# Second channel mixing of the last four tails by seven block products, with the row sums on GpSimd

## The chip, the cores and the metric

The kernel runs on one core of a Trainium2 chip. Its time is the device time of one execution in microseconds, as the median of several runs. The engines are called PE (TensorE), DVE (VectorE), ACT (ScalarE), POOL (GpSimd) and SP (SyncE); the last issues transfers, and so do ACT and POOL. All times below that begin with 2 and have three digits before the point, such as 228.24, are microseconds from the start of the profiled execution.

## The reference

A linear attention is followed by an MLP mixer. Batch 8, 8 heads, 576 tokens, head size 64, so that a token has 512 channels; 256 token units, 1536 channel units.

```python
phi = lambda x: np.where(x > 0, x, np.exp(x) - 1.0) + 1.0
q_p, k_p = phi(q), phi(k)
kv = np.einsum('bhsd,bhse->bhde', k_p, v)
z = np.sum(k_p, axis=2)
x = np.einsum('bhsd,bhde->bhse', q_p, kv) / (np.einsum('bhsd,bhd->bhs', q_p, z)[..., None] + 1e-06)
x = x.transpose(0, 2, 1, 3).reshape(B, S, 512)
h = np.maximum(x.transpose(0, 2, 1) @ w_tok1, 0.0) @ w_tok2
u = x + h.transpose(0, 2, 1)
out = u + np.maximum(u @ w_ch1, 0.0) @ w_ch2        # the channel mixing
```

The change concerns the last product, `@ w_ch2`, for a part of the rows.

## The kernel before

**Tiles.** The 576 tokens of a batch are 64 groups of 9. Of each group 8 tokens go into four row tiles of 128 (`R = 4`), and the ninth, the *tail*, gives 64 rows for each batch; two batches make one tail tile of 128 rows. The batches are worked one after another, with PE kept on one while the other engines prepare the next. The last block is batch 7 together with the tails of the last four batches, 4 to 7: two tail tiles, numbered e = 0 (batches 4 and 5) and e = 1 (6 and 7).

**Channel mixing.** `wc1` and `wc2` hold the two weight matrices; `u` and `ut` are the rows and tails after the token mixing, `cr` the values after the ReLU, 12 blocks of 128 channel units (`NCH = 12`, `KH = 6`), `crp` those of the two tail tiles of the last block, laid over the first half of the free `cr[0]`. The results are read from PSUM by DVE, which adds `u` and writes float32 into `obuf`, eight slots of 512 columns given out in turn by `o_slots`; from there they go to `out`.

**Seven products in place of eight.** For a pair of row tiles `product(n, j, i)` uses Strassen's scheme in Winograd's form: rows in 2 parts, the 1536 units in 2 halves, columns in 2 halves. Each of the products 1 to 7 is six matmuls of 256 columns. Its left sides are the blocks of `cr` or one of four row sums (`winograd`, `row_sums`, kept in `sb`), its right sides blocks of `wc2` or the sums of weights `tb`, made long before. Products 1, 6, 7 and 4 add up in one PSUM bank (X), 5 and 3 in another (Y), 2 stands alone (Z); DVE reads the bank after each product and adds it into one quarter of the output, so that a product that adds into a bank has to wait until the read before it is done. For batch 7, j = 0 and j = 1 are its two pairs of row tiles. In the names of the sequence below, `p40` is product 4 of j = 0.

**The tails before.** `tail_third(e, third)` makes four of a tail tile's 12 matmuls of 512 columns; after the third third, DVE reads the bank once, and SP and ACT each store one batch's 64 rows.

**The order.** The last block is an order written out by hand, the string `SEQUENCE`: `last_block` walks it, and each engine gets its instructions in this order. In it `m` stands for a product of the first channel mixing of batch 7 (`mix_first`), `c` for a sixth of the first mixing of the tails (`mm3_tails`, L570, with its ReLU on ACT at L572), `r` for the four row sums of two blocks on DVE, `q` for a third of a tail and `p` for a product with its read and, where it completes something, its store:

```python
SEQUENCE = """... m23 c3 m27 r0 c4 m24 r2 c5 q00 p10 r4 q01 p20 q02 p60 q10 p50
    q11 p70 q12 p11 p30 p21 p40 p61 p51 p71 p31 p41"""
```

**The stores.** j = 0 is stored as a whole after p40, in two transfers of 256 KB, one from SP and one from ACT (L806); j = 1 in four quarters, after p21, p71, p31 and p41, each as two transfers of 64 KB (L803). The two tail tiles go out after q02 and q12, each as two transfers of 128 KB (L598).

Of the kernel before, what the change touches and what calls it, by code (L numbers as in the profile page):

```python
# [13 lines left out]
ALU = mybir.AluOpType  # L14
# [5 lines left out]
def kernel(  # L20
# [20 lines left out]
    nc = tc.nc  # L41

    B, H, S, D = q.shape
# [3 lines left out]
    R = 4  # L47
    R1 = R + 1
    T = 2 * R + 1
# [5 lines left out]
    NCH = DCH // 128  # L55
# [10 lines left out]
    def bank(at=None):  # L66
        if at is None:
            at, ring[1] = ring[1], (ring[1] + 1) % 4
        return psum[:, at]
# [10 lines left out]
    def const(name, shape, dt=BF16):  # L80
        return consts.tile(shape, dt, name=name, tag=name)
# [6 lines left out]
    wc2 = const("wc2", [128, NCH, DM])  # L88
# [11 lines left out]
    ut = [const(f"ut{i}", [128, DM]) for i in range(2)]  # L100
# [3 lines left out]
    cr = [const(f"cr{b}", [128, NCH, SM]) for b in range(2)]  # L104
# [9 lines left out]
    half = [slice(0, 64), slice(64, 128)]  # L114
# [6 lines left out]
    def after(ins, other):  # L121
        if other is not None:
            tc.add_manual_dep(ins.ins, other.ins.name, sync_dep, reason="order of transfers")
        return ins
# [15 lines left out]
    live = {}  # L140
    o_at = [0]

    def o_slots(m):
        at = o_at[0] if o_at[0] + m <= 8 else 0
        o_at[0] = (at + m) % 8
        return obuf[:, at:at + m]
# [405 lines left out]
    def mm3_tail(p, i):  # L552
# [10 lines left out]
    crp = cr[0].rearrange("p k s -> p (k s)")[:, 0:NCH * 256].rearrange(  # L563
        "p (h k e s) -> p h k e s", h=2, e=2, s=128)
# [21 lines left out]
        if kcs[-1] == NCH - 1 and not wait:  # L586
            mm4_end(p, t)

    def tail_third(e, third):
        ps = bank(2 + e)  # L590
        for kc in range(4 * third, 4 * third + 4):
            nc.tensor.matmul(out=ps, lhsT=crp[:, kc // 6, kc % 6, e], rhs=wc2[:, kc, :],  # L592
                             start=(kc == 0), stop=(kc == NCH - 1))
        if third == 2:
            o = o_slots(2)[:, 0]
            nc.vector.tensor_tensor(out=o, in0=ps, in1=ut[e], op=ALU.add)
            for b, queue in enumerate((nc.sync, nc.scalar)):
                queue.dma_start(out=outv[B - 4 + 2 * e + b, :, 2 * R], in_=o[half[b]])  # L598

    outv = out.rearrange("n (p t) d -> n p t d", t=T)  # L600

    def mm4_end(p, t):
# [25 lines left out]
    KH = NCH // 2  # L628

    def bf(nm, b, i):  # L630
        t = raw[nm, b].rearrange("p j f -> p (j f)").bitcast(BF16)
        return t[:, 1536 * i:1536 * (i + 1)]

    tb = [bf("k", 1, i).rearrange("p (k c) -> p k c", k=KH) for i in range(3)] + [
        bf("q", 1, 0).rearrange("p (k c) -> p k c", k=KH)]
    tf = raw["q", 1].rearrange("p j f -> p (j f)")[:, 768:2304].rearrange("p (k c) -> p k c", k=KH)
    sb = [(bf("v", 1, i) if i < 3 else bf("q", 1, 1)).rearrange("p (k j s) -> p k j s", k=KH, j=2)
          for i in range(4)]
# [4 lines left out]
    def wblock(i, j):  # L643
        return wc2[:, KH * i:KH * (i + 1), 256 * j:256 * (j + 1)]
# [14 lines left out]
    def ablock(n, i, e):  # L659
        return cr[n % 2].rearrange("p k (j e s) -> p k j e s", j=2, e=2)[:, KH * i:KH * (i + 1), :, e]  # L660

    def winograd(s_, a, which, ks):
        a11, a12, a21, a22 = [t[:, ks] for t in a]
        x_, y_, op = {1: (a21, a22, ALU.add), 2: (s_[0][:, ks], a11, ALU.subtract),
                      3: (a11, a21, ALU.subtract), 4: (a12, s_[1][:, ks], ALU.subtract)}[which]
        nc.vector.tensor_tensor(out=s_[which - 1][:, ks], in0=x_, in1=y_, op=op)  # L666

    def row_sums(n, which, k0, m):
        winograd(sb, [ablock(n, i, e) for e in range(2) for i in range(2)], which,
                 slice(k0, k0 + m))  # L670


# [68 lines left out]
    def mix_first(g, i):  # L741
        ps = bank({1: (1, 4, 7), 6: (1, 4, 7), 7: (1, 4, 7), 4: (1, 4, 7), 2: (0, 0, 0),
                   5: (5, 6, 5), 3: (5, 6, 5)}[i][g]).rearrange("p (j c) -> p j c", j=2)
        first = i in (1, 2, 5)
        lhs, rhs = {1: (cblock(0, 0), ublock(0, 0)), 2: (cblock(0, 1), ublock(1, 0)),
                    3: (sw[3], ublock(1, 1)), 4: (cblock(1, 1), tu[3]), 5: (sw[0], tu[0]),
                    6: (sw[1], tu[1]), 7: (sw[2], tu[2])}[i]
        for j in range(2):
            cs = slice(128 * (2 * g + j), 128 * (2 * g + j) + 128)
            for k_ in range(2):  # L750
                nc.tensor.matmul(out=ps[:, j], lhsT=lhs[:, k_, cs], rhs=rhs[:, :, k_],  # L751
                                 start=(first and j == 0 and k_ == 0), stop=(k_ == 1),
                                 skip_group_check=not first or j == 1)
        c1, c6, c5 = hold[g]
        dst = lambda m, e: cr[1][:, KH * m + 2 * g:KH * m + 2 * g + 2, HALF[e]]
        if i == 4:
            nc.scalar.activation(out=dst(1, 0), in_=ps, func=AF.Relu)
        elif i in (1, 6, 5):
            nc.scalar.copy(out={1: c1, 6: c6, 5: c5}[i], in_=ps)
        else:  # L760
            o, c = {2: (dst(0, 0), c1), 3: (dst(0, 1), c6), 7: (dst(1, 1), c5)}[i]
            add_relu(o, ps, c)

    HC = [slice(0, 256), slice(256, 512)]

    def product(n, j, i):
        b = n % 2
        a_ = lambda h, e: ablock(n, h, e)[:, :, j]
        s_ = lambda k_: sb[k_][:, :, j]
        lhs, rhs, tile_, first = {  # L770
            1: (a_(0, 0), wblock(0, 0), "X", True), 2: (a_(1, 0), wblock(1, 0), "Z", True),
            6: (s_(1), tb[1], "X", False), 5: (s_(0), tb[0], "Y", True),
            7: (s_(2), tb[2], "X", False), 4: (a_(1, 1), tb[3], "X", False),
            3: (s_(3), wblock(1, 1), "Y", False)}[i]
        ps = bank({"X": (0, 4), "Z": (6, 5), "Y": (1, 7)}[tile_][j])[:, 0:256]
        for k_ in range(KH):
            nc.tensor.matmul(out=ps, lhsT=lhs[:, k_], rhs=rhs[:, k_], start=(first and k_ == 0),  # L777
                             stop=(k_ == KH - 1), skip_group_check=not first)
        if i == 1:
            live["oj", j] = o_slots(2)  # L780
        o = live["oj", j]
        ur = lambda e, c: u[b][:, 2 * j + e, HC[c]]
        add = lambda e, c, x_, y_: nc.vector.tensor_tensor(out=o[:, e, HC[c]], in0=x_, in1=y_,
                                                           op=ALU.add)
        if i == 1:
            add(0, 0, ps, ur(0, 0))
        elif i == 2:
            add(0, 0, ps, o[:, 0, HC[0]])
        elif i == 6:
            add(0, 1, ps, ur(0, 1))  # L790
        elif i == 5:
            add(1, 1, ps, ur(1, 1))
        elif i == 7:
            add(1, 1, ps, o[:, 1, HC[1]])
        elif i == 4:
            add(1, 0, ps, ur(1, 0))
        elif i == 3:
            add(0, 1, ps, o[:, 0, HC[1]])
        queues = [nc.sync, nc.scalar]
        if j == 1 and i in (2, 7, 3, 4):  # L800
            d, cs = {2: (0, HC[0]), 7: (1, HC[1]), 3: (0, HC[1]), 4: (1, HC[0])}[i]
            for e in range(2):
                queues[e].dma_start(out=outv[n, :, 2 * (2 * j + d) + e, cs], in_=o[half[e], d, cs])  # L803
        elif i == 4:
            for e in range(2):
                queues[e].dma_start(out=outv[n, :, 4 * j + e:4 * j + e + 3:2], in_=o[half[e]])  # L806


    ORDER = [1, 2, 6, 5, 7, 3, 4]
# [26 lines left out]
    def pair_put(n):  # L836
        for e in range(2):
            nc.gpsimd.dma_start(out=outv[n, :, e:e + 7:2], in_=live["o4"][half[e]])

    SEQUENCE = """m01 m02 m11 m05 m15 m06 m12 c0 m21 m03 m16 m07 c1 m25 m13 m22 m17 m04 c2 m26 m14
        m23 c3 m27 r0 c4 m24 r2 c5 q00 p10 r4 q01 p20 q02 p60 q10 p50
        q11 p70 q12 p11 p30 p21 p40 p61 p51 p71 p31 p41"""

    def last_block(n):
        for e in SEQUENCE.split():
            a = [int(c) for c in e[1:]]
            if e[0] == "m":  # L850
                mix_first(*a)
                if e == "m02":
                    pair_end(n - 1, "X", 1, 0)
                    pair_put(n - 1)
            elif e[0] == "c":
                mm3_tails(*a)
            elif e[0] == "p":
                product(n, a[1], a[0])
            elif e[0] == "q":
                tail_third(*a)  # L860
            else:
                for which in range(1, 5):
                    row_sums(n, which, a[0], 2)
# [205 lines left out]
    first = steps(1)  # L1069
# [71 lines left out]
    for n in range(2, B - 1):  # L1141
        p, b = divmod(n, 2)
# [123 lines left out]
```

## Time and profile before

| | |
|---|---|
| median of 8 runs | 249.45 us (248.0 to 250.53) |
| the profiled execution's own time | 248.22 us |
| its span | 246.4 us |
| PE busy | 237.2 us (96%), 2432 matmuls |
| DVE busy | 190.4 us (77%) |
| ACT busy | 139.6 us (57%) |
| POOL busy | 70.8 us (29%) |
| granted PE clock in the last 20 us | 1.00 |
| matmul of 512 columns of `tail_third`, mean | 379 ns |
| matmul of 256 columns of `product`, mean | 272 to 273 ns |
| read of 512 columns, L596 | 692 ns |
| read of 256 columns, L783 | 424 ns |
| row sum of 512 elements on DVE, L666 | 418 to 424 ns |

The span is the time from the first to the last instruction; the execution's own time is 1.8 us longer. A share of busy time is an average over all stages, and matmuls overlap each other, so what one costs is read from the distance between groups of them and not from its mean duration. A line in which several engines are named can be read by columns: start, length, engine, line, operation, output and inputs, how often. In a table by stretches each engine has its busy time and, in brackets, its number of instructions; the granted clock, the busy share of the 16 transfer engines and the rate in GB/s stand at the end.

### The profile page before, as it was taken

The page shows a single profiled execution, that of the slowest core. Times are in us where ns is not written, and L with a number is a line of the kernel's source. Part 1 is how long each engine was busy: PE and PEld are TensorE (multiplying, and loading weights), DVE is VectorE, ACT ScalarE, POOL GpSimd, SP SyncE. Part 2 cuts the span into 40 slices and gives each one's busy share as a digit, 9 for nine tenths or more (in the row PEclk, how much of TensorE's full clock was granted, in tenths as well). Part 3 has the DMA queues.
Part 4 walks back from the last instruction along what each step waited for, and adds up shares of the span by engine and source line. Part 5 has one row for each costly group of instructions (what it writes and reads, how often), then busy time and mean ns, then how long its engine had stood idle before and what let it go on. Part 6 is the DMA issues. An engine that isn't in the chain of part 4 may idle for free.

```text
span 246.4 us, 5963 instructions
## 1 busy us (share of the span) xinstructions
PE 237.2 (96%) x2432; PEld 158.5 (64%) x2454; DVE 190.4 (77%) x330; ACT 139.6 (57%) x224; POOL 70.8 (29%) x84
## 2 busy tenths in 40 slices
PE   7799999999999999999999999999999999999993
PEld 3484455564868556775778445864577566888672
DVE  5955777899799899979894397759884879956753
ACT  4773790669774387736896178655852651266100
POOL 9770040296702700070004500150006700530000
PEclk9999999999999999999999999999999999999999
DMA  6999999999715996599949967799061702361036
GB/s 240 270 203 251 353 277 319 349 257 291 286 24 117 257 381 227 111 250 295 404 125 157 396 182 235 122 346 230 23 136 28 170 3 43 64 130 43 4 85 170
DMA packets 49771, 48.39 MB, mean 196 GB/s; under 512 B 30032, under 2 KB 35536, under 8 KB 49744
## 3 DMA queue, kind: packets, MB, share of 16 engines
q1 hardware_dynamic: 41648, 35.00, 48.0%
q0 software_dynamic: 7472, 12.22, 22.3%
q10 hardware_dynamic: 624, 0.79, 1.1%
q8 instruction: 19, 0.31, 0.6%
q14 instruction: 8, 0.07, 0.1%
HBM read 35.85 MB, written 9.44 MB: 184 GB/s over the span
## 4 chain that ended last, share of the span: by engine, by line
PE 82%; DMA 11%; POOL 3%; issue 1%; DVE 1%; SPq 0%; POOLq 0%
PE ps L823 23%; PE ps L543 21%; DMA wc<-in_moe_w_ch_dram 7%; PE ps L312 6%; PE ps L583 5%; DMA q_raw<-in_q_dram 5%; PE ps L325 4%; PE ps L723 4%; PE ps L751 4%; PE ps L777 4%; PE ps L557 2%; PE ps L570 2%; PE ps L592 2%; PE ps L261 2%; PE ps L191 2%
## 5 line engine op out<-in xcount | busy, mean ns | idle before, releaser
L543 PE MATMUL ps<-uT,wc 128*128 128x512 bf16 x284 | 66.5, 379 | 0.3 <-issue 0.2
L550 ACT ACTIVATE cr<-ps 128x512 bf16<-128x512 f32 x67 | 39.1, 600 | 34.0 <-PE ps L543 33.6
L543 PEld LDWEIGHTS <-wc 128*128 128x128 bf16 x288 | 27.4, 98 | 29.7 <-issue 0.9
L834 POOL TENSOR_TENSOR obuf<-obuf,q_raw 128x512 f32<-128x512 f32 x6 | 7.6, 1269 | 91.2 <-DVE obuf L832 58.6
L823 PE MATMUL ps<-k_raw,v_raw 128*128 128x256 bf16 x216 | 24.9, 273 | 0.0
L832 DVE TENSOR_TENSOR obuf<-ps,u 128x512 f32<-128x512 f32 x24 | 16.2, 687 | 10.4 <-PE ps L823 8.8
L823 PEld LDWEIGHTS <-cr 128*128 128x128 bf16 x216 | 21.1, 98 | 4.1
L823 PEld LDWEIGHTS <-v_raw 128*128 128x128 bf16 x216 | 21.1, 98 | 3.9 <-issue 0.4
L151 ACT ACTIVATE e<-q_raw 128x1152 bf16<-128x1152 f32 x16 | 18.2, 1160 | 7.5 <-DMA q_raw<-in_q_dram 7.5
L151 ACT ACTIVATE e<-k_raw 128x1152 bf16<-128x1152 f32 x16 | 18.2, 1164 | 3.5 <-DMA k_raw<-in_k_dram 3.3
L823 PE MATMUL ps<-wc,cr 128*128 128x256 bf16 x144 | 17.7, 273 | 0.0
L276 DVE TENSOR_TENSOR x<-ps,dens 128x768 bf16<-128x768 f32 x18 | 17.2, 954 | 0.4
L666 DVE TENSOR_TENSOR v_raw<-cr 128x768 bf16<-128x768 bf16 (+2 forms) x24 | 14.8, 619 | 3.2 <-ACT cr L729 2.1
L337 DVE TENSOR_TENSOR u<-ps,x 128x1024 bf16<-128x1024 f32 x12 | 14.6, 1220 | 1.3 <-PE ps L325 1.1
L312 PE MATMUL ps<-x,w 128*128 128x512 bf16 x49 | 13.3, 379 | 0.3
L176 ACT CAST vs<-v_raw 128x1152 bf16<-128x1152 f32 x12 | 13.5, 1160 | 0.0
L165 DVE TENSOR_TENSOR qp<-e,y 128x1152 bf16<-128x1152 bf16 x16 | 11.9, 755 | 1.8 <-ACT e L151 0.8
L157 DVE TENSOR_SCALAR y<-k_raw 128x1152 bf16<-128x1152 f32 x16 | 11.7, 764 | 2.0 <-DMA k_raw<-in_k_dram 1.9
L583 PE MATMUL ps<-wc,cr 128*128 128x512 bf16 x47 | 11.8, 379 | 0.4 <-DMA wc<-in_moe_w_ch_dram 0.3
L834 POOL TENSOR_TENSOR obuf<-obuf,part 128x512 f32<-128x512 f32 x6 | 7.7, 1275 | 15.7 <-DVE obuf L832 15.7
L325 PE MATMUL ps<-ar,w2p 128*128 128x512 bf16 x44 | 11.8, 379 | 0.3
L165 DVE TENSOR_TENSOR kp<-e,y 128x1152 bf16<-128x1152 bf16 x16 | 11.7, 750 | 0.5 <-ACT e L151 0.4
(178 smaller groups left out, 430.3 us busy)
## 6 DMA issues: line engine op xcount, KB each, us to landing
k_raw<-in_k_dram SPq DMA_DIRECT2D x16, 576.0 KB, 6.6
q_raw<-in_q_dram SPq DMA_DIRECT2D x16, 576.0 KB, 5.8
v_raw<-in_v_dram SPq DMA_DIRECT2D x14, 576.0 KB, 10.1
out_dram<-obuf POOLq DMA_DIRECT2D x12, 512.0 KB, 6.6
wc<-in_moe_w_ch_dram POOLq DMA_DIRECT2D x8, 384.0 KB, 10.2
out_dram<-obuf POOLq DMA_DIRECT2D x4, 256.0 KB, 5.1
cr<-in_v_dram POOLq DMA_DIRECT2D x2, 288.0 KB, 7.6
out_dram<-obuf POOLq DMA_DIRECT2D x4, 128.0 KB, 7.9
```

The source lines that it names most:

```text
L151: nc.scalar.activation(out=e, in_=f, func=AF.Exp)
L165: live["phi"] = nc.vector.tensor_tensor(out=dst.transpose([0, 2, 1, 3]), in0=e.rearrange("p (i t d) -> p i t d", i=nj, t=T), in1=y.rearran ...
L276: nc.vector.tensor_tensor(out=xv[:, :, rc0:rc0 + 3], in0=v_[m][:, :, k0:k0 + 6, 0:D].rearrange("p i (q a) d -> p i q a d", a=2), in1=den.r ...
L312: nc.tensor.matmul(out=ps[:, mt], lhsT=w1t[:, b, ms] if r == R else w1[:, r, ms], rhs=x[b][:, r, :], start=(r == 0), stop=(r == R))
L325: nc.tensor.matmul(out=ps[:, i], lhsT=w2v(kt, r, b), rhs=ar[b][:, kt, :], start=(kt == 0), stop=(kt == NT - 1 and not add))
L543: nc.tensor.matmul(out=ps, lhsT=wc1[:, kj, 128 * mc:128 * mc + 128], rhs=uTj[b][:, kj] if n < 2 else uT[b][:, :, kj], start=(kj == 0), sto ...
L550: nc.scalar.activation(out=cr[b][:, mc, :], in_=ps, func=AF.Relu)
L583: nc.tensor.matmul(out=ps, lhsT=crt[:, kc, :] if t == 8 else cr[b][:, kc, 128 * r:128 * r + 128], rhs=wc2[:, kc, :], start=(kc == 0), stop ...
L666: nc.vector.tensor_tensor(out=s_[which - 1][:, ks], in0=x_, in1=y_, op=op)
L823: nc.tensor.matmul(out=live[tile_][:, j], lhsT=lhs[:, k_], rhs=rhs[:, k_], start=(first and j == 0 and k_ == 0), stop=(k_ == KH - 1), skip ...
L832: nc.vector.tensor_tensor(out=o, in0=live[tile_], in1=u[n % 2][:, d::2, HC[c]], op=ALU.add)
L834: nc.gpsimd.tensor_tensor(out=o, in0=o, in1=part[i], op=ALU.add)
```

## The change

The two tail tiles of the last block are treated as one pair of row tiles: their second channel mixing is made by seven products of six matmuls of 256 columns, instead of two tiles of 12 matmuls of 512 columns. The four row sums (`ts`, of 768 elements each, laid over the second half of `cr[0]`) are made by POOL; the first of them waits for the last row sum of batch 7 on DVE. The X bank of the tails is bank 2, Y is 3 and Z is 7. Their results go into two `obuf` slots, and each tail tile is stored as before by two transfers of 128 KB, after products t3 (tile 0) and t4 (tile 1).

In the sequence, `P` is a product's matmuls alone, `R` its read and store, `p` both; `T`, `U` and `t` are the same for the tails' products, where `T10` is the first five and `T11` the sixth matmul of product 1; `s` stands for the four sums on POOL. `r4` now comes ahead of all of batch 7's products, and the reads of p10, p20, p11, p21, p50, p60, p51, p61 and p70 are placed by themselves. The tails' products 1 and 2 come first of all, the other five among the last eight of batch 7.

```diff
-    def tail_third(e, third):
-        ps = bank(2 + e)
-        for kc in range(4 * third, 4 * third + 4):
-            nc.tensor.matmul(out=ps, lhsT=crp[:, kc // 6, kc % 6, e], rhs=wc2[:, kc, :],
-                             start=(kc == 0), stop=(kc == NCH - 1))
-        if third == 2:
-            o = o_slots(2)[:, 0]
-            nc.vector.tensor_tensor(out=o, in0=ps, in1=ut[e], op=ALU.add)
-            for b, queue in enumerate((nc.sync, nc.scalar)):
-                queue.dma_start(out=outv[B - 4 + 2 * e + b, :, 2 * R], in_=o[half[b]])
...
-    def winograd(s_, a, which, ks):
+    def winograd(s_, a, which, ks, engine=nc.vector):
...
-        nc.vector.tensor_tensor(out=s_[which - 1][:, ks], in0=x_, in1=y_, op=op)
+        return engine.tensor_tensor(out=s_[which - 1][:, ks], in0=x_, in1=y_, op=op)
 
     def row_sums(n, which, k0, m):
-        winograd(sb, [ablock(n, i, e) for e in range(2) for i in range(2)], which,
+        live["row"] = winograd(sb, [ablock(n, i, e) for e in range(2) for i in range(2)], which,
                  slice(k0, k0 + m))
...
-        ps = bank({"X": (0, 4), "Z": (6, 5), "Y": (1, 7)}[tile_][j])[:, 0:256]
+        if first:
+            live[tile_, j] = bank({"X": (0, 4), "Z": (6, 5), "Y": (1, 7)}[tile_][j])[:, 0:256]
+        ps = live[tile_, j]
         for k_ in range(KH):
             nc.tensor.matmul(out=ps, lhsT=lhs[:, k_], rhs=rhs[:, k_], start=(first and k_ == 0),
                              stop=(k_ == KH - 1), skip_group_check=not first)
+
+    def product_read(n, j, i):
+        b = n % 2
+        ps = live[{2: "Z", 5: "Y", 3: "Y"}.get(i, "X"), j]
...
+    ta = [crp[:, h, :, e] for e in range(2) for h in range(2)]
+    ts = [cr[0].rearrange("p k s -> p (k s)")[:, 3072 + 768 * i:3840 + 768 * i].rearrange(
+        "p (k s) -> p k s", k=KH) for i in range(4)]
+
+    def tail_sums():
+        for which in range(1, 5):
+            after(winograd(ts, ta, which, slice(0, KH), nc.gpsimd),
+                  live["row"] if which == 1 else None)
+
+    def tail_product(i, ks):
+        lhs, rhs, tile_, first = {
+            1: (ta[0], wblock(0, 0), 2, True), 2: (ta[1], wblock(1, 0), 7, True),
+            6: (ts[1], tb[1], 2, False), 5: (ts[0], tb[0], 3, True), 7: (ts[2], tb[2], 2, False),
+            4: (ta[3], tb[3], 2, False), 3: (ts[3], wblock(1, 1), 3, False)}[i]
+        if ks[0] == 0 and first:
+            live["t", tile_] = bank(tile_)[:, 0:256]
+        ps = live["t", tile_]
+        for k_ in ks:
+            nc.tensor.matmul(out=ps, lhsT=lhs[:, k_], rhs=rhs[:, k_], start=(first and k_ == 0),
+                             stop=(k_ == KH - 1), skip_group_check=not first)
+
+    def tail_read(i):
+        ps = live["t", {1: 2, 2: 7, 5: 3, 3: 3}.get(i, 2)]
+        if i == 1:
+            live["ot"] = o_slots(2)
+        o = live["ot"]
+        e, c, x_ = {1: (0, 0, ut[0]), 2: (0, 0, None), 6: (0, 1, ut[0]), 5: (1, 1, ut[1]),
+                    7: (1, 1, None), 4: (1, 0, ut[1]), 3: (0, 1, None)}[i]
+        nc.vector.tensor_tensor(out=o[:, e, HC[c]], in0=ps,
+                                in1=o[:, e, HC[c]] if x_ is None else x_[:, HC[c]], op=ALU.add)
+        if i in (3, 4):
+            for b, queue in enumerate((nc.sync, nc.scalar)):
+                queue.dma_start(out=outv[B - 4 + 2 * e + b, :, 2 * R], in_=o[half[b], e])
...
-        m23 c3 m27 r0 c4 m24 r2 c5 q00 p10 r4 q01 p20 q02 p60 q10 p50
-        q11 p70 q12 p11 p30 p21 p40 p61 p51 p71 p31 p41"""
+        m23 c3 m27 r0 c4 m24 r2 c5 T10 T20 T11 T21 r4 s P10 R10 P20 P11 P21 P50 U1 U2 R11 P60 R60
+        P51 R50 P61 R20 R21 P70 R51 R61 R70 p30 t6 p71 t5 t7 p40 p31 t3 t4 p41"""
```

`product_read` holds what `product` did after its matmuls, unchanged; in the changed kernel the store of a quarter of j = 1 is line 798, that of j = 0 line 801 and that of a tail tile line 837.

More of the change, by code (lines that the diff above doesn't have):

```diff
@@ L856, in last_block @@
                 mm3_tails(*a)
[L857 to L860, printed above, removed]
+            elif e[0] in "pPR":
+                if e[0] != "R":
+                    product(n, a[1], a[0])
+                if e[0] != "P":
+                    product_read(n, a[1], a[0])
+            elif e[0] in "tTU":
+                if e[0] != "U":
+                    tail_product(a[0], (range(KH - 1), range(KH - 1, KH))[a[1]] if a[1:] else range(KH))
+                if e[0] != "T":
+                    tail_read(a[0])
+            elif e[0] == "s":
+                tail_sums()
             else:
```

## The prediction

> **What bounds the kernel now.** I read the page first (slices, then the chain), then the chain over the last 10 us, and then the output transfers, because the change touches only the last stage. The rows of the slices are tenths busy in 40 equal slices of 6.16 us.
>
> ```profile
> PE   7799999999999999999999999999999999999993
> DMA  6999999999715996599949967799061702361036
> ```
>
> TensorE (PE) is full to the last slice, and the transfer engines, nearly idle around 230 us, are busy again at the very end. The chain of waits, in order of time (start, length, what):
>
> ```profile
> 227.37 0.87 PE ps L570 x8
> ...
> 229.76 0.86 PE ps L592 x4
> 230.63 0.65 PE ps L777 x6
> ...
> 236.70 5.95 PE ps L777 x54
> 242.65 0.02 issue
> 242.67 0.42 DVE obuf L783
> ```
>
> The last mixing of the tails' first layer (L570) ends at 227.37 + 0.87 = 228.24. From there PE runs without a gap to 242.65. A third of a tail (four matmuls of 512 columns, L592) costs 0.86; a product of six matmuls of 256 columns (L777) costs 5.95 / 9 = 0.661. Check: 14 x 0.661 + 6 x 0.86 = 14.41 = 242.65 - 228.24. The last read ends at 243.09, but the span is 246.44: 3.35 us are output transfers and the close. So I look at those: the timeline of the two issuing queues, the issues with their time to landing, what moved in two stretches, and which queue moved it.
>
> ```profile
> 239.16 0.50 ACTq L803 DMA_DIRECT2D out_dram<-obuf  x1
> 239.81 0.73 ACTq L806 DMA_DIRECT2D out_dram<-obuf  x1
> 241.80 2.06 ACTq L803 DMA_DIRECT2D out_dram<-obuf  x3
> ```
>
> ```profile
> out_dram<-obuf ACTq DMA_DIRECT2D x4, 64.0 KB, 2.4
> out_dram<-obuf SPq DMA_DIRECT2D x1, 256.0 KB, 3.2
> out_dram<-obuf ACTq DMA_DIRECT2D x1, 256.0 KB, 4.1
> ```
>
> ```profile
> 241.00:243.25 2.25, 1.64 (x15) 1.19 (x13) 1.37 (x4) 0.00 (x0) 0.00 (x0) 1.00 0.91 220
> 243.25:245.00 1.75, 0.00 (x0) 0.00 (x0) 0.00 (x0) 0.00 (x0) 0.00 (x0) 1.00 0.81 241
> ```
>
> The last two columns are the busy share of the 16 transfer engines and GB/s. Row block j = 0 leaves in one piece after product p40 (2 x 256 KB, issued at 239.81). Its data moves for 2.25 us at 0.91 busy; then the three last quarters of j = 1 (p71, p31, p41; 2 x 64 KB each) move until 245.0. Between 241.1 and 242.4, and again between 242.7 and 243.3, one queue alone is served:
>
> ```profile
> q1 hardware_dynamic: 121, 0.25, 94.9%
> ```
>
> ```profile
> q10 hardware_dynamic: 91, 0.17, 93.1%
> ```
>
> Hence ScalarE's half of p40 (q10) lands 4.1 us after its issue, SyncE's half (q1) after 3.2. So the present end is balanced: PE sets when p41 is issued (243.1 to 243.3), and the transfer engines are just free when it arrives.
>
> **What the Trainium skill says.** "VectorE: DVE Perf Modes", the section on the errata, prices a matmul at 6 + columns cycles of 2.4 GHz: 216 ns for 512, 109 for 256; the trace has 0.86 / 4 = 215 and 0.661 / 6 = 110. "DMA: Bandwidth & Descriptors", Queues, rings and completion order: an engine finishes a packet of one queue before it turns to the next queue; the q1-then-q10 lines agree. "GPSIMD Engine Reference", Key points: GpSimd shares its SBUF interfaces with VectorE, with contention where VectorE has two SBUF inputs. The row sums of VectorE have two, but they end before the new sums start; the product reads have one PSUM and one SBUF input. No trace line here shows such a slowdown.
>
> **PE.** Removed: 24 matmuls of 512 columns, 6 x 0.86 = 5.16. Added: 7 products of 256, 7 x 0.661 = 4.63. All of it lies on the path: -0.53. Twenty-one products from 228.24 end at 242.12. The k-th ends at 228.24 + 0.661 k: p70 is 11th, t6 13th (starts 236.17), p71 14th, t5 15th, t7 16th, p40 17th (239.48), p31 18th, t3 19th (starts 240.14), t4 20th, p41 21st. The first two tail products are split so that block 5, whose ReLU ends about 228.9, is wanted at 229.3: no wait.
>
> **VectorE.** r4's four row sums move ahead of the first reads. Groups follow each other by 1.46 (r0 226.64, r2 228.10), so r4 runs from 229.6 to 231.1; p50, the first user, starts at 232.2. Two 512-column reads of 0.69 become seven of 0.42 (+1.56 busy). Walking the new order at 0.35 to 0.45 per read, R60 waits for its product until 233.6, R70 starts at 235.8, and from p30 on each read follows its product by about 0.1. Every product that adds into a bank finds its read done: p70 (starts 234.85) needs R60, done 234.05, the closest. Cost 0; the cover is 0.8.
>
> **GpSimd.** Four sums of 768 bf16 elements. No such row exists; two neighbours do:
>
> ```profile
> L694 POOL TENSOR_TENSOR k_raw<-wc 128x256 bf16<-128x256 bf16 x6 | 3.8, 668 | 0.0
> ...
> L653 POOL TENSOR_TENSOR k_raw<-wc,q_raw 128x512 bf16<-128x512 bf16 x3 | 3.4, 1170 | 0.0
> ```
>
> Slope 1.96 ns per element, so 1.67 each; started at 231.2 they end at 232.9, 234.6, 236.2, 237.9. Wanted: the second at 236.17, the third at 238.16, the fourth at 240.14. Slack 1.6 or more, cost 0; nothing else stands on GpSimd's queue then. Bounds: 0, and, if each took the longest L653 (1.67 against 1.17, so 2.4), t3 would stall 0.7. Stalls begin at 2.23 each.
>
> **The output transfers.** The tail rows leave before as 2 x 128 KB at 232.9 and again at 237.1, in idle queues. Now they leave at the end. Issues from the reads (product end + 0.1 + 0.42): p21 235.2, p71 238.0, p40 240.03 (was 239.81, +0.22), p31 240.7, t3 241.35, t4 242.0, p41 242.6. From p40 on that is 512 + 128 + 256 + 256 + 128 KB = 1.31 MB instead of 0.92.
> *Pile-up.* p40's data begins 1.25 after issue (as now) and takes 2.25: to 243.55. Behind it stand 0.79 MB. At 241 GB/s that is 3.25, to 246.8; at full share (241 / 0.81 = 298) 2.64, to 246.2. Now data ends at 245.0, so +1.2 to +1.8.
> *A wait on a counter.* The built program's order names, for every DMA of SyncE and ScalarE, one of eight counters taken in turn, and a DMA first waits for the DMA that had its counter before. On ScalarE:
>
> ```
> before: 128 KB c1, 128 KB c3, p21 c5, p40 c7, p71 c1, p31 c3, p41 c5
> after:  p21 c1, p71 c3, p40 c5, p31 c7, t3 c1, t4 c3, p41 c5
> ```
>
> p41 waited for p21, long landed; now it waits for p40. p40's ScalarE half lands at 240.03 + 4.1 = 244.1, so p41 is issued there at 244.15 instead of 243.3: +0.85. Nothing is queued behind it but the close. Its data would come 1.25 later, at 245.4, into the backlog. The two mechanisms overlap, they don't add: the later one rules. Bounds for the end: +0.85 (queues as fast as they ever were) and +2.1 (p40's second half delayed too, by p31 and t3 on the other queue). I take +1.4.
>
> **The sum.** PE's -0.53 is gained but only brings p41's read to 242.5, ahead of a wait. Data ends at 246.4, the span about 247.85, against 246.44 and the profiled run's 248.22, so 249.6 for such a run. That run lies 1.2 below the median of 8 (249.45); on the median the change gives 250.85.
>
> **Rivals.**
> *The PE gain arrives.* If p40 lands within 2.6 us (its halves served side by side), p41 is issued at 242.6 on both queues and the queue is empty by 244.2: end -0.5, 248.95. For it: PE is full, and 0.53 is certain. Against: one queue at a time was served, and 4.1 is measured. It decides once p40 lands by about 243.4, the time at which p41 was issued before; anything earlier is no slower than before.
> *Only the counter wait.* The transfer engines drain 0.79 MB at the speed of the last stretch without its gaps and p41 is just late by its wait: +0.85, 250.3.
> *GpSimd late, or p40's second half late.* Sums of 2.4 stall t3 by 0.7 and push t3, t4 and p41 together; or p40's q10 half lands 0.8 later and takes p41 with it: +2.1, 251.55.
>
> **How the numbers follow.** Pile-up with the wait 0.60 (own range 250.4 to 251.3), only the wait 0.17, the PE gain 0.10, the late case 0.13. The likeliest gives 250.85. Leaving out the PE gain and the top of the late case, about 2 in 10, gives 249.95 to 251.7. Half a per cent, about what a measurement here can tell from none, is 1.25: slower than 250.70 is 0.65 of the first (0.39), nearly all of the late case (0.12) and a little of the second (0.02): 0.53. Faster than 248.20 would need more than PE has to give: 0.02. Between: 0.45.
>
> **What would show it.** In the new profile: 54 and more matmuls without a gap ending near 242.1; the last read near 242.5; ScalarE's last issue of line 798 at 244.1 or later though its data was ready at 242.6; the engines near 0.9 busy from 241.3 to past 246; GpSimd sums of 1.7 and no PE wait on them. Wrong, if ScalarE's p41 is issued at 242.7 and the span is below 246.4, if the busy stretch ends by 245.2, or if PE shows a hole before t6, t7 or t3.

## The result, and the profile after

The changed kernel took 250.19 us (median of 19 runs, 249.16 to 251.24), the kernel before 249.0 us in the same comparison (median of 52 runs). The ratio is 1.0053, with a 95% interval of 1.0037 to 1.0069: slower by half a per cent, some 1.3 us. The profiled execution took 250.27 us, its span is 248.5 us.

Part of the difference between the two spans (2.04 us) has nothing to do with the change. The chain of waits of the changed kernel, in order of time:

```profile
228.17 0.87 PE ps L570 x8
229.04 1.31 PE ps L823 x12
230.35 6.55 PE ps L768 x60
...
242.15 0.67 PE ps L768 x6
242.81 0.02 issue
242.84 0.42 DVE obuf L778
```

The tails' first layer ends at 229.04, in the kernel before at 228.24. Up to there both execute the same instructions. In twelve profiled executions, one for each kernel of the table below, the point lies between 227.93 and 229.46, and it does not follow the kernel: e1 and e2, which differ from the changed kernel only in the stores of the tails, have it at 228.24 and 228.15. In the profile of the changed kernel the shift arises at 83 us, where PE waits 0.86 for a transfer (`uT<-u`) for which it does not wait in the profile of before; in e3 and e5 it is there within the first 50 us. So I measure from this point: its distance to the end of the span, called the *stretch* below. It is 18.20 before and 19.44 after: +1.24, about what the ratio says (0.53% of 249.0 are 1.32).

PE is faster: 21 products take 242.82 - 229.04 = 13.78 where 14 products and six thirds took 14.41, without a hole. But between its last matmul and the end lie 5.66 instead of 3.79. The output transfers tell why. The issues on ScalarE's queue, with start and length:

```profile
240.68 0.68 ACTq L801 DMA_DIRECT2D out_dram<-obuf  x1
241.45 1.16 ACTq L798 DMA_DIRECT2D out_dram<-obuf  x1
242.70 1.97 ACTq L837 DMA_DIRECT2D out_dram<-obuf  x2
245.21 0.47 ACTq L798 DMA_DIRECT2D out_dram<-obuf  x1
```

These are p40, p31, the two tails (t3, t4) and p41. The read of p41 ended at 243.26; ScalarE issued its half at 245.21, two microseconds later. p40's half had landed just then, at 240.68 + 4.5:

```profile
out_dram<-obuf ACTq DMA_DIRECT2D x1, 256.0 KB, 4.5
```

And the transfer engines had no pause. The table by stretches (the last two columns are their busy share and GB/s):

```profile
242.00:243.00 1.00, 0.80 (x8) 0.47 (x5) 0.59 (x2) 0.00 (x0) 0.00 (x0) 1.00 0.95 195
243.00:244.00 1.00, 0.00 (x0) 0.00 (x0) 0.26 (x1) 0.00 (x0) 0.00 (x0) 1.00 1.00 259
244.00:245.00 1.00, 0.00 (x0) 0.00 (x0) 0.00 (x0) 0.00 (x0) 0.00 (x0) 1.00 0.88 263
245.00:246.00 1.00, 0.00 (x0) 0.00 (x0) 0.00 (x0) 0.00 (x0) 0.00 (x0) 1.00 0.99 328
246.00:247.00 1.00, 0.00 (x0) 0.00 (x0) 0.00 (x0) 0.00 (x0) 0.00 (x0) 1.00 0.78 258
```

So both mechanisms that were forecast are in the trace at once: p41 waits, and the engines are full while it waits. One profile can't say which of them costs the time. GpSimd's sums are no part of it:

```profile
232.06 6.55 POOL L655 TENSOR_TENSOR cr<-cr 128x768 bf16<-128x768 bf16 x4 [13.24 <-DVE q_raw L655]
```

The fourth ends at 238.6; t3, its first user, starts at 240.84, and no product of the chain waits for GpSimd.

### The profile page after: what moved, and what is told of

Read it like the earlier page. It is cut to its first block, busy times and chain, and to the rows that moved or that the text cites. A ratio compares the mean times of both kernels' runs of the same rounds, so it can differ in the third digit from the quotient of the medians.

```text
span 248.5 us, 6016 instructions
## 1 busy us (share of the span) xinstructions
PE 237.1 (95%) x2452; PEld 160.2 (64%) x2472; DVE 191.4 (77%) x335; ACT 139.7 (56%) x224; POOL 77.1 (31%) x88
## 4 chain that ended last, share of the span: by engine, by line
PE 64%; DVE 3%; DMA 2%; issue 1%; DVEq 0%
PE ps L854 19%; PE ps L543 17%; PE ps L312 4%; PE ps L712 4%; PE ps L740 4%; PE ps L768 4%; PE ps L325 3%; PE ps L570 2%; DMA uT<-u 2%; PE ps L823 2%; PE ps L261 1%; PE ps L191 1%; PE ps L557 1%; PE ps L583 1%; DVE u L337 1%
## 5 line engine op out<-in xcount | busy, mean ns | idle before, releaser
L863 DVE TENSOR_TENSOR obuf<-ps,u 128x512 f32<-128x512 f32 x24 | 16.2, 687 | 10.4 <-PE ps L854 8.8
L151 ACT ACTIVATE e<-q_raw 128x1152 bf16<-128x1152 f32 x16 | 18.3, 1162 | 6.3 <-DVE den L241 5.1
L151 ACT ACTIVATE e<-k_raw 128x1152 bf16<-128x1152 f32 x16 | 18.2, 1164 | 3.6 <-DMA k_raw<-in_k_dram 3.5
L325 PE MATMUL ps<-ar,w2p 128*128 128x512 bf16 x44 | 11.8, 379 | 0.3
L157 DVE TENSOR_SCALAR y<-q_raw 128x1152 bf16<-128x1152 f32 x16 | 12.0, 765 | 0.0
```

Of the source, the lines that this page charges most:

```text
L151: nc.scalar.activation(out=e, in_=f, func=AF.Exp)
L157: nc.vector.tensor_scalar(out=y, in0=f, scalar1=1.0, scalar2=1.0, op0=ALU.add, op1=ALU.max)
L325: nc.tensor.matmul(out=ps[:, i], lhsT=w2v(kt, r, b), rhs=ar[b][:, kt, :], start=(kt == 0), stop=(kt == NT - 1 and not add))
L863: nc.vector.tensor_tensor(out=o, in0=live[tile_], in1=u[n % 2][:, d::2, HC[c]], op=ALU.add)
```

## The experiments

All numbers of the last stage side by side. "PE" is the time from the end of the tails' first layer to PE's last matmul, "rest" from there to the end of the span; both from one profile each. The ratio is against the kernel before, over many runs.

| kernel | stretch | PE | rest | ratio (95% interval) |
|---|---|---|---|---|
| before | 18.20 | 14.41 | 3.79 | 1 |
| after | 19.44 | 13.78 | 5.66 | 1.0053 (1.0037 to 1.0069) |
| e1 no counter wait | 19.37 | 13.77 | 5.60 | 1.0064 (1.0040 to 1.0088) |
| e2 few bytes | 19.11 | 13.77 | 5.34 | 1.0036 (1.0020 to 1.0053) |
| e3 both | 18.20 | 13.78 | 4.42 | 1.0008 (0.9993 to 1.0023) |
| e4 p40 early | 18.12 | 13.77 | 4.35 | 1.0023 (1.0005 to 1.0041) |
| e5 before, tails late | 19.72 | 14.40 | 5.32 | 1.0060 (1.0039 to 1.0080) |
| e6 e4 with few bytes | 17.68 | 13.77 | 3.91 | 0.9998 (0.9976 to 1.0019) |
| e7 rows | 17.55 | 13.81 | 3.74 | 0.9982 (0.9966 to 0.9998) |
| e8 reads in line | 20.30 | 14.58 | 5.72 | 1.0085 (1.0051 to 1.0120) |
| e9 e3, GpSimd issues | 18.96 | 13.77 | 5.19 | 1.0030 (1.0014 to 1.0046) |
| e10 e7, GpSimd issues | 17.98 | 13.81 | 4.17 | 0.9995 (0.9982 to 1.0009) |

Each stretch is one profile. In the five kernels with the order of the change (after, e1, e2, e3, e9) ScalarE's half of p40 landed 4.4 to 4.5 after its issue, so a difference of 0.07 between two stretches is not told from none. The ratios hold the chance of the earlier stages too. And four of them hold one thing more: in every run of e4, e6, e7 and e10 the execution's own time is 2.1 us longer than its span (2.08 to 2.21), in every run of the other kernels 1.8 (1.73 to 1.86). So some 0.35 us, or 0.14%, of what these four gain in the stretch is lost outside the span; the runs do not show what it is. The mechanisms are read from the stretch, what a kernel is worth from the ratio.

**e1, the counter wait taken away, the bytes kept.**

```diff
-            for b, queue in enumerate((nc.sync, nc.scalar)):
-                queue.dma_start(out=outv[B - 4 + 2 * e + b, :, 2 * R], in_=o[half[b], e])
+            r0 = 64 * (B - 4 + 2 * e)
+            (nc.sync, nc.scalar)[e].dma_start(
+                out=out.rearrange("n (p t) d -> (n p) t d", t=T)[r0:r0 + 128, 2 * R], in_=o[:, e])
```

> The changed kernel, with each tail tile stored by one transfer of 256 KB (tile 0 from SyncE, tile 1 from ScalarE) instead of two of 128 KB. The same bytes at the same places, two issues fewer, so that p41 gets the counters of p71, which has long landed, and no longer those of p40. Theory A (pile-up: the transfer engines have no gap from p40's data on, and the bytes behind it set the end): p41 is issued about 1 us earlier but its data is not, the end stays, ratio to before 1.004 to 1.006 as for the change. Theory B (the counter wait sets the end): p41's data comes earlier, ratio 1.002 or less.

Measured: stretch 19.37, ratio 1.0064. On ScalarE:

```profile
241.90 1.33 ACTq L837 DMA_DIRECT2D out_dram<-obuf  x1
243.32 0.66 ACTq L798 DMA_DIRECT2D out_dram<-obuf  x1
```

p41 goes out at 243.32 - 228.24 = 15.08 after the first layer (16.17 in the changed kernel, 15.06 before), and the end comes only 0.07 earlier in the profile, and no earlier by the ratio, because the engines are full:

```profile
243.00:244.00 1.00, 0.00 (x0) 0.00 (x0) 0.00 (x0) 0.00 (x0) 0.00 (x0) 1.00 0.92 279
244.00:245.00 1.00, 0.00 (x0) 0.00 (x0) 0.00 (x0) 0.00 (x0) 0.00 (x0) 0.97 1.04 374
```

As theory A said: without the wait, the backlog alone keeps the end where it was.

**e2, the bytes taken away, the counter wait kept.**

```diff
-                queue.dma_start(out=outv[B - 4 + 2 * e + b, :, 2 * R], in_=o[half[b], e])
+                queue.dma_start(out=outv[B - 4 + 2 * e + b, :, 2 * R, 256 - 256 * e:264 - 256 * e],
+                                in_=o[half[b], e, 256 - 256 * e:264 - 256 * e])
```

> The changed kernel, with only 8 columns of each tail row stored after t3 and t4 (the other 504 columns of the tail rows are left out of the output): as many transfers and the same counters, but 0.5 MB less to move behind p40. Theory A (pile-up): the backlog is gone and PE's gain shows, ratio about 0.998, span some 0.5 below before. Theory B (counter wait): ScalarE's p41 is still issued only when p40 has landed, 4.1 to 4.5 after p40's issue, ratio 1.002 to 1.004.

Measured: stretch 19.11, ratio 1.0036. p41 is issued at 244.26 - 228.15 = 16.11, as in the changed kernel, and now the transfer engines run empty while it waits (0.30 busy in the last row):

```profile
243.00:244.00 1.00, 0.00 (x0) 0.00 (x0) 0.00 (x0) 0.00 (x0) 0.00 (x0) 1.00 0.80 231
244.00:245.00 1.00, 0.00 (x0) 0.00 (x0) 0.00 (x0) 0.00 (x0) 0.00 (x0) 0.53 0.30 53
```

As theory B said. Each mechanism is nearly enough by itself: taking one away gains 0.07 or 0.33, since the other holds the end.

**e3, both taken away** (one transfer for each tile, 8 columns of it).

> Both edits: one transfer for each tail tile and only 8 columns of it stored (the other 504 columns of the tail rows are left out). Neither backlog nor counter wait. Both theories: PE's gain of 0.5 to 0.6 shows in full, ratio 0.997 to 0.999. If it is 1.002 or more, the loss is not in the stores but in PE, VectorE or GpSimd.

Measured: stretch 18.20, ratio 1.0008: 1.24 gained, where the single edits give 0.40 in sum. But the expected PE gain of 0.6 isn't there: the rest is 4.42, not 3.79. On ScalarE:

```profile
241.82 1.15 ACTq L798 DMA_DIRECT2D out_dram<-obuf  x1
243.06 1.31 ACTq L837 DMA_DIRECT2D out_dram<-obuf  x1
244.47 0.48 ACTq L798 DMA_DIRECT2D out_dram<-obuf  x1
```

The read of p41 ends at 243.62, and SyncE issues its half at 243.65. ScalarE's goes out at 244.47, because the two issues ahead of it take 1.15 and 1.31 instead of about 0.5, the second for 4 KB. I had not counted on that, but it is not what holds the end: in e9 this half goes out 0.8 earlier and lands at the same time. What is left is p40 itself, which PE's gain does not reach. In the new order p40 is issued 241.04 - 229.41 = 11.63 after the first layer, as before (239.81 - 228.24 = 11.57), its half on ScalarE lands 4.4 later instead of 4.1, and p41 lands behind it, 17.0 after the first layer (17.15 before):

```profile
out_dram<-obuf ACTq DMA_DIRECT2D x1, 64.0 KB, 2.0
```

That is p41's half on ScalarE, 244.47 + 2.0.

**e4, p40 earlier, all output stored.**

```diff
-        P51 R50 P61 R20 R21 P70 R51 R61 R70 p30 t6 p71 t5 t7 p40 p31 t3 t4 p41"""
+        P51 R50 P61 R20 R21 P70 R51 R61 R70 p30 t6 p40 t5 t7 p71 t3 t4 p31 p41"""
```

> The changed kernel with the last products in another order: p30 t6 p40 t5 t7 p71 t3 t4 p31 p41. All of the output is stored; p40's 512 KB are issued about 2 us earlier, so the backlog is worked off before the end, and p41's counter is that of p71. Both theories: p41's data is moved some 1.2 after its issue, ratio 0.997 to 0.999, faster than both kernels. If the loss were on PE or GpSimd (t3 now starts 0.66 earlier, t5 and t7 too): a hole in PE before t3, ratio above 1.000.

Measured: stretch 18.12, ratio 1.0023. 1.32 of the stretch come back, but not the PE gain. PE has no hole. From p40 on even 128 KB more are moved than in the changed kernel, those of p71, and the engines are full from 239 to 244:

```profile
242.00:243.00 1.00, 0.00 (x0) 0.00 (x0) 0.21 (x1) 0.00 (x0) 0.00 (x0) 1.00 0.95 303
243.00:244.00 1.00, 0.00 (x0) 0.00 (x0) 0.00 (x0) 0.00 (x0) 0.00 (x0) 1.00 0.87 289
```

The expectation missed that: p41's data is ready, and still queues. That the ratio is above 1 though the stretch is no longer than before is in part the 0.35 us outside the span.

**e5, the late stores alone**, in the kernel before, with its own tail matmuls:

```diff
-c5 q00 p10 r4 q01 p20 q02 p60 q10 p50
-        q11 p70 q12 p11 p30 p21 p40 p61 p51 p71 p31 p41"""
+c5 q00 p10 r4 q01 p20 p60 q10 p50
+        q11 p70 p11 p30 p21 p61 p51 p71 p40 p31 q02 q12 p41"""
```

> The kernel before, with its own tails (thirds of 512 columns, no sums, no products), only their last thirds and thus their stores moved behind p31: one part of the change alone, the late stores. I read the stretch from the end of the tails' first layer on PE to the end of the span: 18.2 before, 19.5 after. If the loss comes from the stores' place: 19.3 to 19.9, ratio 1.004 to 1.007, with PE as before (14.4). If it comes from the products, the sums on GpSimd or the reads: 18.2 to 18.5, ratio within 0.002 of 1.

Measured: stretch 19.72, ratio 1.0060, PE 14.40. The edit moves one thing more than the expectation names: p40 goes behind p61, p51 and p71, where the change has it too. Since two thirds of the tails have left the way ahead of it, it is issued at nearly the same time, 11.8 after the first layer instead of 11.6. As in the changed kernel, ScalarE's p41 goes out only when p40's half has landed, at 245.84, 16.4 after the first layer. Seven products, GpSimd's sums and the placing of the reads are all absent, and the loss is there in full, 1.52. It is the place of the stores: the tails' behind p40, at the end.

**e6, e4 without the tails' bytes** (8 columns of each row):

> The order of e4 with only 8 columns of each tail row stored (the other 504 columns of the tail rows are left out): neither backlog, nor counter wait, nor a slow issue ahead of p41. The stretch from the end of the tails' first layer to the end should be 17.5 to 17.7 (18.2 before, 18.1 in e4), PE's gain of 0.6 in full. If it stays at 18.1, e4 isn't held by its transfers but by the close after the last product.

Measured: stretch 17.68, ratio 0.9998. Of PE's 0.63, 0.52 show in the stretch, about as expected, so e4 is held by the bytes of its tails. The main difference from e3 is that p40 goes out two microseconds earlier, and that brings most of what e3 lacked. The ratio shows none of it; 0.35 is lost outside the span.

**e7, a version that stores early.** Row tile 0 of j = 0 leaves after p30, and the three smallest stores are last:

```diff
-        elif i == 4:
+        elif j == 0 and i in (3, 4):
             for e in range(2):
-                queues[e].dma_start(out=outv[n, :, 4 * j + e:4 * j + e + 3:2], in_=o[half[e]])
+                queues[e].dma_start(out=outv[n, :, 2 * (i - 3) + e], in_=o[half[e], i - 3])
...
-        P51 R50 P61 R20 R21 P70 R51 R61 R70 p30 t6 p71 t5 t7 p40 p31 t3 t4 p41"""
+        P51 R50 P61 R20 R21 P70 R51 R61 R70 p30 t6 t5 p40 t7 t3 t4 p71 p31 p41"""
```

with e1's store of the tails.

> All of the output is stored. The changed kernel with row tile 0 of j = 0 stored after p30 and row tile 1 after p40, the order p30 t6 t5 p40 t7 t3 t4 p71 p31 p41, and one transfer for each tail tile. The last three stores are the small quarters, and their counters belong to transfers issued 4 us or more before. Stretch 17.6 to 17.9, ratio 0.996 to 0.999. If the backlog still binds: 18.1, as e4.

Measured: stretch 17.55, ratio 0.9982 (0.9966 to 0.9998), median 248.56 us. As expected it is faster than the changed kernel, and than the kernel before by 0.18%, with an interval that ends just below 1. The biggest transfer now lands in 2.2, and the last three in as much:

```profile
out_dram<-obuf ACTq DMA_DIRECT2D x1, 256.0 KB, 2.2
out_dram<-obuf ACTq DMA_DIRECT2D x3, 64.0 KB, 2.2
```

**e8, the placing of the reads undone.**

```diff
-r4 s P10 R10 P20 P11 P21 P50 U1 U2 R11 P60 R60
-        P51 R50 P61 R20 R21 P70 R51 R61 R70 p30 t6 p71 t5 t7 p40 p31 t3 t4 p41"""
+r4 s p10 p20 p11 p21 p50 U1 U2 p60
+        p51 p61 p70 p30 t6 p71 t5 t7 p40 p31 t3 t4 p41"""
```

> The changed kernel with each read back behind its product, only r4 kept ahead: the placing of the reads undone. My theory: the reads had 0.8 of slack, PE has no gap either way, and the end is that of the stores: stretch 19.3 to 19.6 as after, ratio 1.004 to 1.007. Rival: the placing is what keeps PE full; without it PE shows holes and the stretch is over 19.8.

My theory failed here; the rival is right. Stretch 20.30, PE 14.58, which is 0.80 more. PE's timeline has a hole ahead of p51; in brackets the idle time and whom PE waited for, line 833 being a read of the tails:

```profile
235.08 1.14 PE L768 MATMUL ps<-k_raw,v_raw 128*128 128x256 bf16 x9 [0.65 <-DVE obuf L833]
```

Bank 7 is used twice: for the tails' product 2 and then for p51. With the reads in line, U2 is the seventh read after the row sums and ends at 235.02; p51 has to wait for it. In the changed kernel U2 is third and ends at 233.04, 1.2 before p51 needs the bank (eight products of 0.656 after 229.04, at 234.29). So the placing is worth 0.8 of PE's time. The rest of the 20.30 is the stores, as in the changed kernel (5.72 and 5.66).

**e9, e3 with the two small stores issued by GpSimd** (`nc.gpsimd` in place of the two queues):

> As e3 (8 columns of each tail row stored, one transfer for each tail tile; the other 504 columns of the tail rows are left out), but the two small stores are issued by GpSimd instead of SyncE and ScalarE. In e3 ScalarE issued p41 at 15.1 after the tails' first layer, 0.85 after its read was done, behind two issues of 1.15 and 1.31 (0.5 elsewhere), without backlog or counter wait. If the long issues queued ahead held p41: it is issued at 14.25 now and the stretch falls from 18.2 to 17.5 to 17.8. If it was the traffic itself, the stretch stays at 18.1 to 18.3.

p41 goes out when expected, at 243.62 - 229.37 = 14.25 after the first layer:

```profile
243.62 0.76 ACTq L798 DMA_DIRECT2D out_dram<-obuf  x1
```

So in e3 its issue was held by the issues queued ahead of it. But it lands no earlier than in e3:

```profile
out_dram<-obuf ACTq DMA_DIRECT2D x1, 64.0 KB, 2.8
```

243.62 + 2.8 is 17.05 after the first layer, 244.47 + 2.0 in e3 was 17.06. So, as far as one profile of each can tell, the rival is right: it was the traffic. That the stretch even grew, to 18.96, has another reason. GpSimd's own drain at the close (shortest, median and longest, first and last start) begins at 243.2, takes 4.33 and ends at 247.5, the last of all:

```profile
L1302 POOLq DRAIN  x3: 51/102/4331, 243.2 to 248.0; - x3
```

The gain would not have come through without it either. At the close SyncE waits for the stores; it reached its own drain at 246.8, 17.4 after the first layer, and in e3 at 246.7, which is 17.3 and 0.9 before the end. By that, e9 would have ended at some 18.3 without GpSimd's drain, an estimate, where the expectation has 18.1 to 18.3 for traffic.

**e10, e7 with GpSimd issuing the tails.**

> As e7 (all of the output stored), but the two tail tiles are issued by GpSimd. If the queues of SyncE and ScalarE are still in the way in e7, the stretch falls below 17.5; if PE and the last transfer alone set the end there, it stays at 17.5 to 17.7, or grows where GpSimd's transfers land later than p41's.

Measured: stretch 17.98, ratio 0.9995, worse than e7 (0.9982), though the intervals overlap. PE is as in e7; the rest grew from 3.74 to 4.17. GpSimd's transfers landed in 2.5, well before p41's. Its drain took 4.33 again, but here it was over at 246.1:

```profile
L1302 POOLq DRAIN  x3: 51/93/4334, 241.8 to 247.0; - x3
```

SyncE reached its own drain later, at 246.4, 0.9 before the end, as in e7 (244.6). So the drain is not the cause here. ScalarE's p41 goes out 14.47 after the first layer in both kernels, but the three quarters on its queue land in 2.6 (median) where e7 has 2.2. Why they are slower was not separated.

## Why the prediction was right, point by point

*PE.* Forecast -0.53, measured 13.78 - 14.41 = -0.63; a product costs 0.656. The split of the tails' first two products left no gap, as said.

*VectorE.* No hole, as forecast. The sentence that every product "that adds into a bank finds its read done" came true, but it looks only at such products and leaves out a bank that is given to another product (7); there e8 shows that 0.8 hang on the placing of the reads.

*GpSimd.* Forecast 1.67 for a sum, measured 6.55 for four, or 1.64; no wait. The first one started at 3.0 after the tails' first layer in the trace (232.06), as forecast (231.2 - 228.24).

*Pile-up and counter wait.* "The two mechanisms overlap, they don't add: the later one rules": e1, e2 and e3 show it, with 0.07 and 0.33 gained by the single edits and 1.24 by both. Counted from the first layer, ScalarE's p41 was forecast at 15.9 and issued at 16.2, since p40's half landed in 4.5 and not 4.1. The lines on q1 and q10 show that one half was served alone before the other; they show no end of a packet, so that the rule named there is the cause is not shown. The last data left somewhat earlier than the forecast 18.2: the engines are done in the bin that ends at 247, at most 18.0.

*The sum.* Forecast +1.4, measured +1.24 in the stretch and 0.53% in the ratio. The forecast 250.85 was counted from a median of 249.45; the larger set of runs puts the kernel before at 249.0, which is most of the distance to 250.19.

*The rivals.* "The PE gain arrives" needed p40 landed by 243.4, on the clock of the kernel before; it landed at 245.2, which is 244.4 on that clock. The condition was well chosen: counted from the first layer it is 15.2, p40 landed at 16.0 in e3, without the gain, and at 13.7 in e6, with it. It was not enough by itself, though: in e4 p40 landed at 13.7 too, and the tails' bytes still stood in the way. "Only the counter wait" is refuted by e1, the late case by the +1.24: GpSimd's sums made nobody wait, and p40's second half was late by 0.4, not 0.8.

*What was missing.* That a gain on PE must reach the largest store to count. The order of the change leaves p40's issue where it was, so that with the wait and the tails' bytes both taken away (e3) the end is only as early as before. And that an issue itself grows longer behind unserved transfers; in e3 this delays p41's issue, and e9 shows that it does not delay its landing.

## What to carry to other kernels

At the end of a kernel, PE's time is worth only what the last store lets through: count the bytes behind the largest store, and put the small ones last and the large ones early. A gain that doesn't bring the largest store forward did not move the end here (e3); with that store two microseconds earlier it did (e6, e7). When transfers take their completion counters in turn, look up whose counter the last one gets; a large store four places before it on the same queue becomes its wait. Where one limit hides another, single edits show almost nothing (0.07 and 0.33 here) and only both together show the size (1.24).

## What the runs showed of the hardware that I had not expected

Issuing a transfer from ScalarE took 0.50 with little in flight. For the two stores that follow p40's 512 KB, the first after 0.8 to 0.9 us, it took 1.10 to 1.33 in the changed kernel, e1, e2, e3 and e5, even for 4 KB (e3), and what is queued behind on that engine is issued late by as much; that it also lands late was not seen (e3 and e9). It isn't a fixed price: in e8 the first of the two took 0.56 and the second 1.82. Where the next store came two microseconds after p40 (before, e4, e6), the quarters behind it took 0.5 to 0.75.

In e3 the small stores behind p40 landed one at a time: the two stores of 4 KB and p41's two of 64 KB, issued between 242.43 and 244.47, landed at 245.8, 246.0, 246.2 and 246.4, some 0.2 apart for either size.

GpSimd's drain at the close took 4.33 in both kernels in which it issues stores, of 4 KB (e9) or of 256 KB (e10). In e9 it ended 1.1 after the last store had landed (246.4) and was the last of all; in e10 it began earlier and was over in time. Without stores of its own (e1, e3, e7) it took 6.10, but began at 234 to 236 and was long over.
